# RWKV attention with a top-1 expert router: the order of rows and maskings in the attention's steps, and the attention's end written out step by step

## The chip, the core and the metric

The kernel runs on one core of a Trainium2 chip. The metric is the time of one execution on the device in microseconds. Before the change it is 439.42 us, the median of three runs (438.77 to 440.31). The profile is of one further execution, whose span is 438.4 us.

A core has five engines that work side by side, each with its own instruction queue, kept in order: TensorE (PE; the loads of its weights are shown apart as PEld), VectorE (DVE), ScalarE (ACT), GpSimd (POOL) and SyncE (SP), which starts transfers. Results of TensorE land in PSUM; everything else lives in SBUF. An engine that waits holds up all that stands behind it in its queue, so the order in which a program lists its operations is part of its speed.

## What is computed

Inputs are r, k, v of shape (4, 8, 768, 48) (batch, heads, sequence, head size), a decay w and a bonus u per head and channel. The attention is a recurrence over the sequence; its rows, 3072 of 384, then go through a router that sends each to one of eight experts.

```python
for t in range(S):
    kt, vt, rt = k[:, :, t], v[:, :, t], r[:, :, t]
    cur = einsum('bhd,bhe->bhde', u[None] * kt, vt)
    y[:, :, t] = einsum('bhd,bhde->bhe', rt, state + cur)
    state = w[None, :, :, None] * state + einsum('bhd,bhe->bhde', kt, vt)
x = y.transpose(0, 2, 1, 3).reshape(B * S, H * D)          # (3072, 384)

xn, en = x / (norm(x) + 1e-6), expert_emb / (norm(expert_emb) + 1e-6)
logits = xn @ en.T / tau
expert_idx = argmax(logits); gate_w = softmax(logits)[expert_idx]
for e in range(E):                                          # E = 8, F = 1024
    mask = expert_idx == e
    out[mask] = gate_w[mask, None] * (relu(x[mask] @ w1[e]) @ w2[e])
```

## The kernel before

The sequence is cut into six chunks of 128 positions; a unit is one chunk of one batch, 24 units in all. The loop below runs over the units; each pass works on several of them at different stages. Inside a unit the attention is matrix work: scores (`at`) of all pairs of positions, masked to the earlier ones (`AT`); sums (`y`) of the values weighted by the masked scores and, from the second chunk on, of the state that is carried from chunk to chunk (`st`, `state`); the term of the bonus u, which is a row scaling of v (`diag`, `xd`). `rows` turns the sums back (`yrows`) and adds `xd` to them: that is `X`, the rows that the router and the experts take. Heads go in pairs of 64 rows, of which 48 are used; the 16 rows between are the gaps that the diff speaks of.

```python
B, H, S, D = 4, 8, 768, 48
C, NCH, DP, NP, PP = 128, 6, 64, 4, 112        # PP = DP + D
...

def own_rows(k, i, half):
    if half == 0:
        k.xd[i] = k.work.tile([128, H, D], F32, name="xd", tag="xd")
    diag, V = k.diag[i], k.loaded[i][2]
    for h in range(half * H // 2, (half + 1) * H // 2):
        k.nc.scalar.mul(k.xd[i][:, h, :], V[:, h, :], diag[:, h : h + 1])

def turn_k(k, i):
    nc = k.nc
    Kw = k.Kpad[i % len(k.Kpad)]
    kt = k.ps.tile([128, NP, C], F32, name="kt", tag="tp")
    for p in range(NP):
        nc.tensor.transpose(kt[:, p, :], pair(Kw, p), k.ident)
    k.KT[i] = k.work.tile([128, NP, C], F32, name="KT", tag="KT")
    nc.scalar.copy(k.KT[i], kt)

def scores(k, i):
    nc = k.nc
    RT, KT = k.RT[i], k.KT.pop(i)
    at = [k.ps.tile([128, NP, C], F32, name="at", tag="at") for _ in range(2)]
    for p in range(NP):
        for s in range(2):
            rows = slice(s * DP, s * DP + D)
            nc.tensor.matmul(at[s][:, p, :], KT[rows, p, :], RT[rows, p, :], start=True, stop=True)
    k.AT[i] = []
    for s in range(2):
        a = k.work.tile([128, NP, C], F32, name=f"AT{s}", tag=f"AT{s}")
        nc.vector.tensor_mul(a, at[s], k.umask[:, None, :].to_broadcast([128, NP, C]))
        k.AT[i].append(a)

...

def sums(k, i):
    nc = k.nc
    mm = nc.tensor.matmul
    c, b = divmod(i, B)
    V, RT, AT, T = k.loaded[i][2], k.RT.pop(i), k.AT.pop(i), k.state[b]
    y = [k.ps.tile([128, NP // 2, C], F32, name="y", tag="y") for _ in range(2)]
    for q in range(NP // 2):
        for u in range(2) if c > 0 else ():
            for s in range(2):
                mm(
                    y[s][u * DP : (u + 1) * DP, q, :], T[s * DP : s * DP + D, 2 * q + u, :],
                    RT[s * DP : s * DP + D, 2 * q + u, :], start=(q == 0), stop=False, skip_group_check=True,
                )
    for s in range(2):
        for q in range(NP // 2):
            for u in range(2):
                p = 2 * q + u
                mm(
                    y[s][u * DP : u * DP + D, q, :], V[:, 2 * p + s, :], AT[s][:, p, :],
                    start=(c == 0 and q == 0), stop=True, skip_group_check=True,
                )
        yT = k.yT[i % len(k.yT)]
        if c > 0:
            nc.scalar.copy(yT[0:PP, s], y[s][0:PP])
        else:
            for u in range(2):
                heads = slice(u * DP, u * DP + D)
                nc.scalar.copy(yT[heads, s], y[s][heads])
    if b == 0:
        k.groups[c] = group(k, c)

def rows(k, i):
    nc = k.nc
    c, b = divmod(i, B)
    yT = k.yT[i % len(k.yT)]
    y = k.ps.tile([128, 2, NP // 2, 2 * DP], F32, name="yrows", tag="tp")
    for s in range(2):
        for q in range(NP // 2):
            nc.tensor.transpose(y[:, s, q, 0:PP], yT[0:PP, s, q, :], k.ident[0:PP, 0:PP])
    def by_bank(t):
        return t.rearrange("t (g s) d -> t s g d", s=2)
    X = k.groups[c].X[:, b, :].rearrange("t (h d) -> t h d", d=D)
    nc.vector.tensor_add(
        by_bank(X), y.rearrange("t s q (u d) -> t s (q u) d", d=DP)[:, :, :, 0:D], by_bank(k.xd.pop(i))
    )
```

PSUM tiles come from pools with few buffers: two each for the tags `tp`, `at` and `y`, one for every other tag.

After each chunk its 512 rows are routed: logits, the choice of an expert, the place of each row in its expert's list (`ranks`, `places`), the list entries (`gates`, `listed`, `taken`, `summed`). After the fourth chunk the two experts with the most rows are settled, their weights loaded and the first 128 rows of each gathered, so that these two tiles (`Early`) can be computed while the last two chunks are routed. The loop runs seven passes past the last unit, in which the stages of the last chunks drain and the early tiles are worked off in halves:

```python
def attention(k):
    units = B * NCH
    def on(f, i, *more):
        if 0 <= i < units:
            f(k, i, *more)
    ...                                        # of_group, whole: the same by units and by chunks of a group
    for i in range(-1, units + 7):
        j = i - SETTLED * B                    # SETTLED is 3
        ...
        on(turn_r, i + 1)
        on(own_rows, i, 0)
        on(turn_k, i + 1)
        whole(turn_logits, i - 3)
        on(scaled, i + 2)
        for n in (0, 1) if i < 0 else (i + 2,):
            on(own, n)
        on(states, i)
        of_group(squares, i - 1)
        on(own_rows, i, 1)
        whole(norms, i - 2)
        whole(choose, i - 3)
        whole(before, i - 3)
        whole(exps, i - 4)
        whole(located, i - 4)
        whole(gates, i - 5)
        whole(listed, i - 5)
        on(own_sum, i + 1)
        if j == 10:
            k.lists = turned_lists(k, perm, "st")
            lists = taken_by_rank(k, k.lists)
            first = [Early(k, r, *lists, w) for r, w in zip(LAST, k.weights)]
        on(sums, i)
        on(carry, i)
        on(scores, i + 1)
        on(rows, i)
        of_group(put, i)
        of_group(turn_rows, i - 1)
        whole(logits, i - 2)
        whole(ranks, i - 3)
        if i == units:
            first[0].hidden(0)
        whole(taken, i - 5)
        ...
        if j == 7:
            load_, count = loads(k, "st")
        if j == 8:
            settle(k, load_, count)
            for w, r in zip(k.weights, LAST):
                load_weights(k, expert_number(k, r), w)
        if j == 9:
            perm = turner(k, k.by)
        if j == 10:
            to = outs(k, lists[0], E * TM)
        ...         # passes past the last unit, and what follows: see the diff

class Early:        # its rows are gathered when it is made
    ...
    def turn(self):
        k, nc = self.k, self.k.nc
        ps = k.ps.tile([128, NK, 128], F32, name="early_x", tag="tp")
        for m in range(NK):
            nc.tensor.transpose(ps[:, m, :], self.G[:, m * 128 : (m + 1) * 128], k.ident)
        self.xT = k.work.tile([128, NK, 128], F32, name="earlyx", tag="KU")
        nc.vector.tensor_copy(self.xT, ps)
    ...             # hidden, rows, out: see the lines taken away in the diff
```

When all lists are known (`lists`, `taken_by_rank`), the rest of each expert's rows is gathered and the experts run one after the other (`experts`, not changed).

## Time and profile before

| what | value |
|---|---|
| time, median of three | 439.42 us |
| span of the profile | 438.4 us |
| TensorE busy | 404.5 us, 92% |
| first scores start | 15.27 us |
| scores of the last unit start | 147.41 us |
| first transpose of the experts' rows (L1055) | 188.81 us |
| last gathers of early rows land, early_x starts | 155.09 and 156.51 us |

The page gives the busy time of each engine, the span in 40 slices, the transfers and the chain that ended last. In its forty slices, with the engines' busy share in tenths, three regimes can be told apart: the attention up to slice 14 (each slice is 11 us), the end of the attention with the early tiles up to slice 17, and the experts:

```profile
PE   8889999999998877998999999999999999999960
...
ACT  2477776666677610133323323143233233232110
POOL 6875677676755210440032140222221231300200
PEclk9999999999999969999999999999999999999995
```

A busy TensorE isn't a TensorE at its peak, and a wait that is listed for an engine is put down to whichever releaser came last by the profile; where the engine named had long been done, it was another one. In a timeline, "xN" at the end of a line merges N instructions, and the bracket says how long the engine idled before it and what ended the idling.

### The profile page before, as it was taken

The numbers are of one execution on the slowest core, as the hardware profiler recorded it, in microseconds if no ns is written. First come the engines' busy times: TensorE is split into PE (matmuls) and PEld (weight loads), VectorE is DVE, ScalarE is ACT, GpSimd is POOL, SyncE is SP. The second block draws the span as 40 slices with busy tenths as digits, with TensorE's granted clock in tenths as the row PEclk, the third lists the DMA queues.
The fourth block names the chain that finished last, engine by engine and source line by source line (L and its number), as shares of the span: only waits on it lengthen the run. The fifth ranks groups of instructions, "written<-read, shape, count | busy, mean of one in ns | idle before, by whom it ended". The sixth has DMA issues, their size and how long they took to land.

```text
span 438.4 us, 9319 instructions
## 1 busy us (share of the span) xinstructions
PE 404.5 (92%) x3556; PEld 357.2 (81%) x3556; DVE 251.0 (57%) x610; ACT 176.6 (40%) x531; POOL 161.4 (37%) x218
## 2 busy tenths in 40 slices
PE   8889999999998877998999999999999999999960
PEld 3667778787887764878999999999999999899660
DVE  4566776767678723255776776355556566566210
ACT  2477776666677610133323323143233233232110
POOL 6875677676755210440032140222221231300200
PEclk9999999999999969999999999999999999999995
DMA  8966656666641980234452643155155151230110
GB/s 165 180 145 145 141 122 139 130 129 145 144 93 42 365 299 1 67 94 146 146 175 65 234 138 144 37 167 175 59 167 196 37 165 52 63 135 2 52 41 21
DMA packets 93801, 54.40 MB, mean 124 GB/s; under 512 B 76937, under 2 KB 88380, under 8 KB 93746
## 3 DMA queue, kind: packets, MB, share of 16 engines
q1 hardware_dynamic: 89024, 43.85, 37.5%
q0 software_dynamic: 3296, 9.44, 6.7%
q8 instruction: 30, 0.49, 0.4%
q10 hardware_dynamic: 1426, 0.41, 0.4%
q14 instruction: 25, 0.20, 0.2%
HBM read 44.45 MB, written 9.63 MB: 123 GB/s over the span
## 4 chain that ended last, share of the span: by engine, by line
PE 77%; DVE 7%; POOL 4%; ACT 4%; issue 3%; DMA 2%; POOLq 0%; DVEq 0%; ACTq 0%
PE ps L1107 22%; PE ps L1171 16%; PE ps L1211 5%; PE at L344 4%; PE ps L1224 4%; PE y L400 3%; PE early_h L920 3%; PE wake L67 3%; DVE AT L348 2%; PE ps L1085 2%; PE ps L1055 2%; PE kt L332 2%; PE early_y L931 2%; PE y L392 2%; PE st L363 2%
## 5 line engine op out<-in xcount | busy, mean ns | idle before, releaser
L1231 POOL DMA_INDIRECT out_dram<-y,to x25 | 30.0, 1200 | 179.5 <-issue 93.1
L1107 PE MATMUL ps<-xTe,w 128*128 128x192 f32 (+3 forms) x336 | 62.9, 327 | 0.0
L1107 PEld LDWEIGHTS ps<-xTe,w 128*128 128x128 f32 x336 | 55.9, 190 | 0.4
L312 ACT ACTIVATE xd<-V,diag 128x48 f32<-128x48 f32 x192 | 48.3, 325 | 0.2 <-DVE diag L303 0.2
L348 DVE TENSOR_TENSOR AT<-at,umask 128x512 f32<-128x512 f32 x48 | 30.9, 686 | 29.4 <-PE at L344 29.4
L1114 ACT ACTIVATE hT<-hT 128x384 f32<-128x384 f32 (+3 forms) x42 | 22.0, 523 | 33.8 <-DVE hT L1137 21.1
L1171 PE MATMUL ps<-Tw,Sh 128*128 128x192 f32 x192 | 32.5, 326 | 0.0
L1171 PEld LDWEIGHTS ps<-Tw,Sh 128*128 128x128 f32 x192 | 31.4, 190 | 0.0
L973 POOL DMA_INDIRECT G<-xs,take x25 | 27.1, 1083 | 8.8 <-issue 3.4
L344 PE MATMUL at<-RT,KT 48*128 48x128 f32 x384 | 27.9, 284 | 2.0 <-DVE RT L323 0.9
L1107 PE MATMUL ps<-Tx,Sw 128*128 128x192 f32 (+3 forms) x168 | 29.6, 326 | 0.0
L344 PEld LDWEIGHTS at<-RT,KT 48*128 48x128 f32 x384 | 23.3, 187 | 6.6 <-ACT xd L312 2.8
L1107 PEld LDWEIGHTS ps<-Tx,Sw 128*128 128x128 f32 x168 | 27.6, 190 | 0.1
L400 PE MATMUL y<-AT,V 128*48 128x128 f32 x384 | 25.8, 277 | 0.0
L1124 DVE TENSOR_TENSOR u<-ps,p 128x384 f32<-128x384 f32 (+3 forms) x14 | 7.8, 556 | 31.4 <-PE ps L1107 30.6
L511 ACT COPY xT<-xp 128x384 f32<-128x384 f32 x24 | 11.5, 479 | 35.2 <-PE xp L509 35.2
L297 POOL TENSOR_TENSOR KU<-KU,Rpad 128x384 f32<-128x384 f32 x24 | 24.1, 1003 | 1.9
L296 POOL TENSOR_TENSOR KU<-K,u_bc 128x384 f32<-128x384 f32 x24 | 24.1, 1002 | 0.0
L288 POOL TENSOR_TENSOR Kpad<-K,kpow 128x384 f32<-128x384 f32 x23 | 23.0, 999 | 2.8 <-DVE kpow L101 2.8
L1171 PE MATMUL ps<-w,hT 128*128 128x192 f32 x128 | 23.4, 326 | 0.0
L400 PEld LDWEIGHTS y<-AT,V 128*48 128x48 f32 x384 | 19.8, 123 | 3.4 <-issue 3.4
L1171 PEld LDWEIGHTS ps<-w,hT 128*128 128x128 f32 x128 | 21.3, 190 | 0.3
(240 smaller groups left out, 816.6 us busy)
## 6 DMA issues: line engine op xcount, KB each, us to landing
w<-in_moe_w_dram SPq DMA_DIRECT2D x16, 1536.0 KB, 6.8
K<-in_k_dram SPq DMA_DIRECT2D x24, 192.0 KB, 4.1
V<-in_v_dram SPq DMA_DIRECT2D x24, 192.0 KB, 4.3
xs<-X SPq DMA_DIRECT2D x24, 192.0 KB, 2.0
Rpad<-in_r_dram SPq DMA_DIRECT2D x23, 192.0 KB, 4.2
G<-xs,take POOLq DMA_INDIRECT x27
out_dram<-y,to POOLq DMA_INDIRECT x25
Rpad<-in_r_dram ACTq DMA_DIRECT2D x1, 192.0 KB, 4.2
```

Of the source, the lines that this page charges most:

```text
L288: k.nc.gpsimd.tensor_mul(k.Kpad[i % len(k.Kpad)][:, :, 0:D], k.loaded[i][0], k.kpow)
L296: nc.gpsimd.tensor_mul(KU, K, k.u_bc)
L297: nc.gpsimd.tensor_mul(KU, KU, R[:, :, 0:D])
L312: k.nc.scalar.mul(k.xd[i][:, h, :], V[:, h, :], diag[:, h : h + 1])
L344: nc.tensor.matmul(at[s][:, p, :], KT[rows, p, :], RT[rows, p, :], start=True, stop=True)
L348: nc.vector.tensor_mul(a, at[s], k.umask[:, None, :].to_broadcast([128, NP, C]))
L400: mm(y[s][u * DP : u * DP + D, q, :], V[:, 2 * p + s, :], AT[s][:, p, :], start=(c == 0 and q == 0), stop=True, skip_group_check=True,)
L973: nc.gpsimd.indirect_dma_start(out=G[0:n, :], out_offset=None, in_=k.xs[:, :], in_offset=IndirectOffsetOnAxis(ap=take[0:n], axis=0), bound ...
L1107: nc.tensor.matmul(ps[:, j, :], weights[:, (f + j) * 128 : (f + j + 1) * 128], moving, start=(first and j == 0), stop=True, skip_group_che ...
L1114: nc.scalar.activation(h, h, ACT.Relu)
L1171: nc.tensor.matmul(ps, a[:, f, :], b[:, f, :], start=(first and f == 0), stop=(f == NF // 2 - 1), skip_group_check=True)
L1231: k.nc.gpsimd.indirect_dma_start(out=k.out[:, :], out_offset=IndirectOffsetOnAxis(ap=k.to[0:here, j : j + 1], axis=0), in_=y[0:here, :], i ...
```

## The change

It has five parts.

1. The masking of the scores, one vector operation per set of heads, leaves `scores` and becomes `masked`. The pass now lists: scores of the next unit, its first masking, the rows of this unit (`rows`, with the addition that makes X), the second masking. The addition stood behind both maskings before; the purpose is to read the transposed rows out of PSUM earlier.
2. The gaps between heads: the state tiles shrink from 64 to 48 columns per pair, and products that write 48 of 64 rows now take 64 columns of the operand (the next head's first columns) where the gap would otherwise stay unwritten. So in the first chunk, too, one copy per bank reads all 112 rows, where there were two per bank.
3. The last unit's scaling `xd` is one product on GpSimd, made a pass earlier, instead of eight on ScalarE.
4. The loop ends with the last unit. What followed in seven further passes is written out in the order wanted.
5. The early tiles become a generator of single steps (three products into one slice of `hT`, or one product of the output rows); `fill(n)` puts n of them between two stages of routing. ScalarE scales the early rows, not VectorE.

```diff
--- before.py
+++ after.py
...
@@ -312,6 +312,11 @@
         k.nc.scalar.mul(k.xd[i][:, h, :], V[:, h, :], diag[:, h : h + 1])
+def own_rows_once(k, i):
+    k.xd[i] = k.work.tile([128, H, D], F32, name="xd", tag="xd")
+    k.nc.gpsimd.tensor_mul(k.xd[i], k.loaded[i][2], k.diag[i][:, :, None].to_broadcast([128, H, D]))
@@ -342,11 +347,13 @@
...
-    k.AT[i] = []
-    for s in range(2):
-        a = k.work.tile([128, NP, C], F32, name=f"AT{s}", tag=f"AT{s}")
-        nc.vector.tensor_mul(a, at[s], k.umask[:, None, :].to_broadcast([128, NP, C]))
-        k.AT[i].append(a)
+    k.at[i] = at
+def masked(k, i, s):
+    a = k.work.tile([128, NP, C], F32, name=f"AT{s}", tag=f"AT{s}")
+    k.nc.vector.tensor_mul(a, k.at[i][s], k.umask[:, None, :].to_broadcast([128, NP, C]))
+    k.AT.setdefault(i, []).append(a)
@@ -359,9 +366,9 @@
     st = k.ps.tile([128, NP, D], F32, name="st", tag="st")
     for p in range(NP):
         for s in range(2):
-            h = 2 * p + s
+            h, n = 2 * p + s, (DP, D)[s]
             nc.tensor.matmul(
-                st[s * DP : (s + 1) * DP, p, :], Kw[:, h, :], V[:, h, :], start=True, stop=True, skip_group_check=True
+                st[s * DP : s * DP + n, p, :], Kw[:, h, 0:n], V[:, h, :], start=True, stop=True, skip_group_check=True
             )
     k.st[i] = st
...
@@ -385,29 +392,27 @@
     mm = nc.tensor.matmul
     c, b = divmod(i, B)
     V, RT, AT, T = k.loaded[i][2], k.RT.pop(i), k.AT.pop(i), k.state[b]
+    V, T = (a.rearrange("q h d -> q (h d)") for a in (V, T))
     y = [k.ps.tile([128, NP // 2, C], F32, name="y", tag="y") for _ in range(2)]
     for q in range(NP // 2):
         for u in range(2) if c > 0 else ():
             for s in range(2):
+                p, n = 2 * q + u, (DP, D)[u]
                 mm(
-                    y[s][u * DP : (u + 1) * DP, q, :], T[s * DP : s * DP + D, 2 * q + u, :],
-                    RT[s * DP : s * DP + D, 2 * q + u, :], start=(q == 0), stop=False, skip_group_check=True,
+                    y[s][u * DP : u * DP + n, q, :], T[s * DP : s * DP + D, p * D : p * D + n],
+                    RT[s * DP : s * DP + D, p, :], start=(q == 0), stop=False, skip_group_check=True,
                 )
     for s in range(2):
         for q in range(NP // 2):
             for u in range(2):
-                p = 2 * q + u
+                p, n = 2 * q + u, DP if c == 0 and u == 0 else D
+                h = 2 * p + s
                 mm(
-                    y[s][u * DP : u * DP + D, q, :], V[:, 2 * p + s, :], AT[s][:, p, :],
+                    y[s][u * DP : u * DP + n, q, :], V[:, h * D : h * D + n], AT[s][:, p, :],
                     start=(c == 0 and q == 0), stop=True, skip_group_check=True,
                 )
         yT = k.yT[i % len(k.yT)]
-        if c > 0:
-            nc.scalar.copy(yT[0:PP, s], y[s][0:PP])
-        else:
-            for u in range(2):
-                heads = slice(u * DP, u * DP + D)
-                nc.scalar.copy(yT[heads, s], y[s][heads])
+        nc.scalar.copy(yT[0:PP, s], y[s][0:PP])
...
@@ -805,7 +810,7 @@
             f(k, k.groups[i // B])
     emb = build_experts(k)
-    for i in range(-1, units + 7):
+    for i in range(-1, units):
         j = i - SETTLED * B
@@ -815,7 +820,8 @@
         on(turn_r, i + 1)
-        on(own_rows, i, 0)
+        if i < units - 1:
+            on(own_rows, i, 0)
         on(turn_k, i + 1)
         whole(turn_logits, i - 3)
         on(scaled, i + 2)
@@ -823,7 +829,8 @@
         on(states, i)
         of_group(squares, i - 1)
-        on(own_rows, i, 1)
+        if i < units - 1:
+            on(own_rows, i, 1)
@@ -832,6 +839,8 @@
         whole(gates, i - 5)
         whole(listed, i - 5)
         on(own_sum, i + 1)
+        if i == units - 2:
+            own_rows_once(k, i + 1)
         if j == 10:
             k.lists = turned_lists(k, perm, "st")
@@ -839,13 +848,13 @@
         on(sums, i)
         on(carry, i)
         on(scores, i + 1)
+        on(masked, i + 1, 0)
         on(rows, i)
+        on(masked, i + 1, 1)
         of_group(put, i)
         of_group(turn_rows, i - 1)
         whole(logits, i - 2)
-        if i == units:
-            first[0].hidden(0)
         whole(taken, i - 5)
@@ -863,28 +872,51 @@
             perm = turner(k, k.by)
         if j == 10:
             to = outs(k, lists[0], E * TM)
-        if i == units - 1:
-            for f in first:
-                f.turn()
-        if i == units + 1:
-            first[0].hidden(1)
-        if i == units + 2:
-            first[0].rows(0)
-        if i == units + 4:
-            first[0].rows(1)
-            load_, _ = loads(k, "xp")
-            first[0].out(to)
-            first[1].hidden(0)
+    g, h = k.groups[NCH - 2], k.groups[NCH - 1]
+    early = itertools.chain(*(f.steps(to) for f in first))
+    def fill(count):
+        for _ in range(count):
+            next(early, None)
+    gates(k, g)
+    first[0].turn()
+    turn_rows(k, h, B - 1)
+    listed(k, g)
+    squares(k, h, B - 1)
+    norms(k, h)
+    logits(k, h)
+    first[1].turn()
+    logits_out(k, h)
+    fill(1)
+    turn_logits(k, h)
+    choose(k, h)
+    before(k, h)
+    taken(k, g, "tp")
+    fill(2)
+    ranks(k, h)
+    load_, _ = loads(k, "xp")
+    places(k, h)
+    exps(k, h)
+    located(k, h)
+    summed(k, g)
     by = order(k, load_, k.settled)
-    lists = turned_lists(k, turner(k, by), "xp")
-    first[1].hidden(1)
+    perm = turner(k, by)
+    gates(k, h)
+    listed(k, h)
+    fill(4)
+    taken(k, h, "tp")
+    summed(k, h)
+    fill(1)
+    lists = turned_lists(k, perm, "xp")
     k.take, k.gates = taken_by_rank(k, lists)
     k.rows_of = {r: gathers(k, r) for r in LAST}
     k.to = outs(k, k.take, E * TM)
-    first[1].rows(0)
-    first[1].rows(1)
-    first[1].out(to)
     caps_passed(k, load_, by)
+    for _ in early:
+        pass
 class Early:
@@ -911,35 +943,31 @@
         self.xT = k.work.tile([128, NK, 128], F32, name="earlyx", tag="KU")
         nc.vector.tensor_copy(self.xT, ps)
-    def hidden(self, half):
-        k, nc = self.k, self.k.nc
-        ps = k.ps.tile([128, NF // 2, 128], F32, name="early_h", tag="at")
-        fs = slice(half * NF // 2, (half + 1) * NF // 2)
-        for j, f in enumerate(range(fs.start, fs.stop)):
+    def steps(self, to):
+        k, nc, half = self.k, self.k.nc, NF // 2
+        for f in range(NF):
+            if f % half == 0:
+                ps = k.ps.tile([128, half, 128], F32, name="early_h", tag="at")
             for m in range(NK):
                 nc.tensor.matmul(
-                    ps[:, j, :], self.weights[0][:, m, f * 128 : (f + 1) * 128], self.xT[:, m, :],
+                    ps[:, f % half, :], self.weights[0][:, m, f * 128 : (f + 1) * 128], self.xT[:, m, :],
                     start=(m == 0), stop=(m == NK - 1),
                 )
-        nc.scalar.activation(self.hT[:, fs, :], ps, ACT.Relu)
-
-    def rows(self, half):
-        k = self.k
-        if half == 0:
-            self.ps = k.ps.tile([128, DM], F32, name="early_y", tag="y")
-        for f in range(half * NF // 2, (half + 1) * NF // 2):
-            k.nc.tensor.matmul(
-                self.ps, self.hT[:, f, :], self.weights[1][:, f, :], start=(f == 0), stop=(f == NF - 1)
-            )
-
-    def out(self, to):
-        k, nc, ps = self.k, self.k.nc, self.ps
-        y = k.work.tile([128, DM], F32, name="earlyy", tag="xd")
-        nc.vector.tensor_scalar_mul(y, ps, self.gate)
-        nc.gpsimd.indirect_dma_start(
-            out=k.out[:, :], out_offset=IndirectOffsetOnAxis(ap=to[:, self.col], axis=0), in_=y[:, :], in_offset=None,
-            bounds_check=N - 1, oob_is_err=False,
-        )
+            if f % half == half - 1:
+                nc.scalar.activation(self.hT[:, f - half + 1 : f + 1, :], ps, ACT.Relu)
+            yield
+        ps = k.ps.tile([128, DM], F32, name="early_y", tag="y")
+        for f in range(NF):
+            nc.tensor.matmul(ps, self.hT[:, f, :], self.weights[1][:, f, :], start=(f == 0), stop=(f == NF - 1))
+            if f == NF - 1:
+                y = k.work.tile([128, DM], F32, name="earlyy", tag="xd")
+                nc.scalar.mul(y, ps, self.gate)
+                nc.gpsimd.indirect_dma_start(
+                    out=k.out[:, :], out_offset=IndirectOffsetOnAxis(ap=to[:, self.col], axis=0), in_=y[:, :],
+                    in_offset=None, bounds_check=N - 1, oob_is_err=False,
+                )
+            yield
...
```

More of the change, by code (lines that the diff above doesn't have):

```diff
@@ L138, in build_consts @@
     for b in range(B):
-        t = k.aconst.tile([128, NP, DP], F32, name=f"state{b}")
+        t = k.aconst.tile([128, NP, D], F32, name=f"state{b}")
         nc.gpsimd.memset(t, 0.0)
@@ L374, in carry @@
         return
-    part = T[:, :, 0:D]
-    nc.vector.tensor_add(part, part, st)
-    nc.gpsimd.tensor_mul(part, part, k.wC)
+    nc.vector.tensor_add(T[0:PP], T[0:PP], st[0:PP])
+    nc.gpsimd.tensor_mul(T[0:PP], T[0:PP], k.wC[0:PP])
 def sums(k, i):
@@ L652, in listed, with taken @@
     g.lane, g.what = slices(k, g.c, k.slots.rearrange("p e t -> p (e t)"), *g.spots)
-def taken(k, g):
-    g.take = k.ps.tile([2 * QS, 128], F32, name="take", tag="st")
+def taken(k, g, tag="st"):
+    g.take = k.ps.tile([2 * QS, 128], F32, name="take", tag=tag)
     for b in range(B):
@@ L1443 @@
     n.Rpad, n.Kpad, n.state = [], [], []
-    for name in ("loaded", "KU", "diag", "xd", "RT", "KT", "AT", "st", "y", "groups"):
+    for name in ("loaded", "KU", "diag", "xd", "RT", "KT", "at", "AT", "st", "y", "groups"):
         setattr(n, name, {})
```

## The prediction

> **What bounds the kernel now.** I read the page first, then the waits of TensorE from 38 to 189 us, then the timeline of single steps, and last the tail with its clock. The page's first part says that TensorE is the engine to watch:
>
> ```profile
> PE 404.5 (92%) x3556; PEld 357.2 (81%) x3556; DVE 251.0 (57%) x610; ACT 176.6 (40%) x531; POOL 161.4 (37%) x218
> ```
>
> From 189 us on nothing in the experts is edited, so the 249.6 us from there to the end (438.4 - 188.8) move as one block. All is decided before. There PE idles little; the waits, whose columns are total us, times and longest, are:
>
> ```profile
> PE early_x L910 <- DMA G<-xs,take: 1.9, 2, 1.4
> PE kt L332 <- DVE X L429: 1.9, 3, 0.6
> PE rank L578 <- DVE seq L556: 1.3, 1, 1.3
> PE yrows L423 <- ACT yT L406: 1.3, 1, 1.3
> PE kt L332 <- POOL KU L297: 1.1, 2, 0.6
> PE take L658 <- POOL what L643: 1.0, 1, 1.0
> PE kt L332 <- DVE at L585: 0.9, 4, 0.2
> ```
>
> The three rows of kt sum to 3.9 us over nine steps, and are one wait. The timeline of a plain step (start, duration, engine) shows it:
>
> ```profile
> 60.60 0.60 PE L423 MATMUL yrows<-ident,yT 112*128 112x112 f32 x4
> 60.70 1.29 DVE L348 TENSOR_TENSOR AT<-at,umask 128x512 f32<-128x512 f32 x2 [1.35 <-PE at L344]
> ...
> 61.37 0.60 PE L321 MATMUL rt<-ident,Rpad 128*128 128x128 f32 x4
> ...
> 61.90 0.55 DVE L429 TENSOR_TENSOR X<-yrows,xd 128x384 f32<-128x384 f32 x1
> ...
> 62.59 0.63 PE L332 MATMUL kt<-ident,Kpad 128*128 128x128 f32 x4 [0.63 <-DVE X L429]
> ```
>
> The tag tp has two PSUM buffers and three users per step (rt, kt, yrows), so kt takes the buffer of the yrows before it and needs X to have read that. X stands behind both maskings AT; it ends at 62.45 and kt starts 0.14 us later. At 109.81 the view names POOL's KU, but X ended at 109.66 there: the same wait. Where logits or lists lie between (lgT 0.8 us, take 0.6 us), PE arrives later and waits for nothing.
>
> In the first chunk another wait rules: four copies of yT instead of two.
>
> ```profile
> 30.59 1.53 ACT L410 COPY yT<-y 48x256 f32<-48x256 f32 x4
> ...
> 32.17 0.41 PE L423 MATMUL yrows<-ident,yT 112*128 112x112 f32 x2 [0.37 <-ACT yT L410]
> ```
>
> The tail's clock (columns: stretch, length, busy us of PE, PEld, DVE, ACT, POOL, granted clock, DMA share, GB/s):
>
> ```profile
> 152.00:154.00 2.00, 1.01 (x7) 0.71 (x7) 0.52 (x1) 1.17 (x6) 0.00 (x0) 1.00 1.02 404
> 154.00:156.00 2.00, 0.90 (x3) 0.50 (x3) 0.03 (x1) 0.73 (x3) 0.00 (x0) 0.52 1.03 396
> 156.00:158.00 2.00, 1.49 (x7) 1.52 (x8) 1.14 (x3) 0.00 (x0) 0.00 (x0) 0.50 1.03 373
> 158.00:160.00 2.00, 2.00 (x12) 2.00 (x11) 1.19 (x5) 0.48 (x1) 0.65 (x2) 0.50 1.07 372
> 160.00:162.00 2.00, 2.00 (x15) 1.94 (x14) 0.00 (x0) 0.00 (x0) 1.10 (x2) 0.77 0.97 345
> ```
>
> PE pauses for the gathered early rows, comes back at half speed, and needs until about 161. DMA is full with the experts' weights there.
>
> **What the skill says.** "TensorE: Matmul & The Clock Gate", section "What's actually happening": the clock is halved after an idle window of some 3.4 us and needs about as long a busy one to come back. The trace agrees: 0.52 and 0.50 after the pause, full again from 162. Its "Part 4: PE-mode transpose" adds that transposes don't count as busy in the same way, and all of PE's work from 151.4 to 157.6 is transposes. "GPSIMD Engine Reference", "1. Specifications": no PSUM access, and SBUF interfaces shared with VectorE. The product moved to POOL has both inputs in SBUF, so it can go there; the same form takes 1.00 us (L296). "Perfetto Trace Analysis", "Optimization Strategy": a bubble that repeats can mean too few buffers for the next tile. The tp bubble is this; the change releases the buffer earlier instead of adding one.
>
> **The change part by part.**
>
> *X between the maskings.* AT takes 0.69 us alone and the next vector op starts about 0.55 us after it, so in the step above X can start when yrows is there, at 61.30, instead of 61.90, and ends at 61.85; kt starts at 61.99. By PE's own pace (0.49 us after rt's start, as at 121.12 and 121.61) it could at 61.86: 0.13 us stays. So the four plain steps (three of 0.63, and 109.81) gain 0.50 each, the four with rank (0.23 each) all of it, as PE comes later there, and that at 133.41 0.45: 2.0 + 0.9 + 0.45 = 3.4 us. The second masking ends where X ended; it is wanted 2.4 us later. PE is then the bound: work between score starts is 5.86 - 0.63 = 5.23 us. ACT has a loop beside it: xT, four xd, KT, squares, four xd, two yT, then PE's yrows and xp. By the starts of consecutive ops that is about 5.0 us. It fits, barely. POOL has 3.5 us per step plus at most 1.2, DVE under 5.
>
> *First chunk.* Two copies of 112 rows take 0.62 to 0.74 us, four of 48 took 1.52. A copy of 48 rows costs what one of 112 does (0.367 against 0.362 us), so this halves. Tracking the step starts: kt at 22.44 moves to 21.83 by X; yrows of the next unit, whose second half ended at 27.05, ends at 25.7 (gain 1.35); those after are set by ACT's loop of 5.0 us where they took 5.5: ends at 30.6 (was 32.58) and 35.5 (was 38.11). kt at 38.93 then starts at 36.2: gain 2.7 us. The weights of 64 instead of 48 columns for half of these sums are loaded under other matmuls.
>
> *Narrow states.* Half of the 16 weight loads of st have 48 columns for 64. 20 steps, estimated at 0 to 0.05 us each: 0.4 us. Additions and products keep their 192 columns: nothing.
>
> *Rows of the last unit on POOL.* Eight scalings (0.32 us each) leave ACT; before, PE waited 1.28 us for yT behind four of them. Yet the next PE work is early_x, which waits for the gather. POOL's product needs diag (ends at 148.0) and stands ahead of the gathers: the first is issued at about 149.07 instead of 148.62. So 1 us is won ahead of a wait, and the wait ends 0.45 us later.
>
> *The tail.* Its work is the same: 32 early steps of 0.69 us (3 matmul sums of 0.23, or one of 0.69), 22 us, plus the routing. From the gather's landing (155.1) to the first expert transpose (188.8) PE idled 0.5 + 0.4 + 0.8 + 1.3 + 1.0 + 0.7 = 4.7 us. In the new order I count: 0.45 for the copy xT ahead of lgT, no wait for lg, seq or the fourth chunk's list, 2.4 ahead of the last take, 0.6 at the end. The 2.4 comes from DVE: rank is read at 164.2, then 0.3 + 0.45 + 0.6 + 0.25 + 0.3 + 0.65 + 0.5 + 0.55 + 0.95 us of loads, places, exps, spots, summed, order, perm, gates and slices, and 0.95 on POOL, gives 169.5, while four filled steps last until 167.0. So 3.5 us idle for 4.7, minus the gather's 0.45, and real matmuls now come between transposes while the clock is low, perhaps 0.6 more at half speed. Tail: 0.1 us gained.
>
> **Sum.** 2.7 + 3.4 + 0.4 + 0.1 = 6.6 us; 439.4 - 6.6 = 432.8 us, 1.5% less.
>
> **Rivals.** (1) ACT becomes the bound of the steps. Its loop of 5.0 us against 5.23 leaves 0.2; if starts slip, yrows waits and a third of the 3.4 goes: 434. For it: ACT already stands with no pause from squares to yT. Against: it waits 0.3 us for kt in each step, which shrinks. (2) The tail gives more: if PE, without the gap at 151.4 to 152.7, keeps its clock, some 3 us of half speed vanish and the time is 429.5. Against: the pause itself moves from 1.4 to 2.7 us at one place. (3) The tail gives it back: a low clock for one window longer (1.7 us), or the later gathers under 400 GB/s of weights landing late: 435. (4) DVE's settling at 138 to 141, which kept the scores at 141.75 waiting 0.91 us for RT, could grow if it starved take or lists; I see the same amount of DVE work there, so nothing.
>
> **Range and chances.** Of the 6.6 us, 6.1 rest on waits read off directly, with about 1 us of doubt each for chunk 0 and the steps; the tail has about 2. Together some 2.7 us: 432.8, 429.2 to 436.4. Faster by 2% means under 430.6, which needs the tail to give over 2 us: 0.22. Slower by 2% would need a new serial wait: 0.03.
>
> **What would show it.** kt's wait for X at or under 0.15 us per step; score starts 5.2 to 5.3 us apart in plain steps; ACT's yT twice 0.36 us from the first unit, and kt of the fifth step near 36.2; the scores of the last unit near 141.0 instead of 147.4; early_x first at 149.2 or so, about 8.1 us after them (7.7 before); the last take waiting some 2 us for what; the first expert transpose near 182.2. I am wrong if yrows waits for yT in every step, if the clock in the tail is not low or low for longer, or if PE waits for the rows of the last unit from POOL.

## The result, and the profile after

The changed kernel takes 428.86 us in the median of four runs (428.64 to 430.65), the kernel before 439.87 in the runs beside it. The ratio is 0.976, with a 95% interval of 0.972 to 0.980. The prediction was 432.8 us with a range of 429.2 to 436.4: the median lies 0.3 us below the range's lower end, and 11.0 us were gained where 6.6 were expected.

The first line of the page (busy time, share and instructions of each engine) shows that TensorE has as many instructions as before and that its pauses are fewer: 27 us of the span are not busy, where it was 34:

```profile
PE 399.8 (94%) x3556; PEld 355.6 (83%) x3556; DVE 251.1 (59%) x608; ACT 171.5 (40%) x517; POOL 161.8 (38%) x219
```

The waits of TensorE between 38 and 180 us (total, times, longest) have no row of kt left. In the tail the waits for seq (1.3 us) and for lgT (0.8 us) are gone too, and the wait of take for what has grown from 1.0 to 2.0 us:

```profile
PE early_x L942 <- DMA G<-xs,take: 2.2, 1, 2.2
PE take L663 <- POOL what L648: 2.0, 1, 2.0
PE at L349 <- ACT yT L415: 1.0, 1, 1.0
PE yrows L428 <- ACT yT L415: 1.0, 1, 1.0
PE ps L1083 <- ACT earlyy L965: 0.7, 1, 0.7
```

The timeline of a plain step shows X between the maskings, and kt 0.65 us after the start of rt, where it was 1.22:

```profile
55.62 0.69 DVE L355 TENSOR_TENSOR AT<-at,umask 128x512 f32<-128x512 f32 x1 [0.88 <-PE at L349]
...
56.22 0.56 DVE L434 TENSOR_TENSOR X<-yrows,xd 128x384 f32<-128x384 f32 x1
56.28 0.60 PE L326 MATMUL rt<-ident,Rpad 128*128 128x128 f32 x4
...
56.70 0.68 DVE L355 TENSOR_TENSOR AT<-at,umask 128x512 f32<-128x512 f32 x1
...
56.93 0.63 PE L337 MATMUL kt<-ident,Kpad 128*128 128x128 f32 x4
```

In the first chunk two copies of 112 rows stand where four of 48 stood, and one group of transposes follows them:

```profile
27.83 0.63 ACT L415 COPY yT<-y 112x256 f32<-112x256 f32 x2
...
28.24 0.68 PE L428 MATMUL yrows<-ident,yT 112*128 112x112 f32 x4
```

The clock of the tail (stretch, length, busy us of PE, PEld, DVE, ACT, POOL, granted clock, DMA share, GB/s) is low for half as long as before:

```profile
146.00:148.00 2.00, 1.22 (x12) 0.79 (x12) 0.71 (x2) 0.39 (x2) 0.00 (x0) 1.00 1.02 383
148.00:150.00 2.00, 1.85 (x20) 1.37 (x21) 0.65 (x2) 0.87 (x4) 1.27 (x3) 0.50 1.06 371
150.00:152.00 2.00, 2.00 (x16) 1.83 (x16) 0.75 (x2) 0.00 (x0) 0.48 (x1) 0.64 1.07 374
152.00:154.00 2.00, 2.00 (x24) 1.83 (x18) 1.36 (x8) 0.00 (x0) 0.00 (x0) 1.00 0.58 212
```

Starts in the timelines give the stages, in us:

| stage | before | after | difference |
|---|---|---|---|
| start to the first scores | 15.27 | 13.95 | -1.32 |
| to the scores of unit 5 (chunk 0) | 26.43 | 23.73 | -2.70 |
| to the scores of unit 23 (steps) | 105.71 | 100.79 | -4.92 |
| to early_x | 7.69 | 8.23 | +0.54 |
| to the first expert transpose | 33.71 | 30.72 | -2.99 |
| to the end (experts) | 249.59 | 249.38 | -0.21 |
| span | 438.4 | 426.8 | -11.6 |

The start of early_x is that of its first transposes, at 155.10 us before; those of the second early tile start at 156.51 there. The first row is not the change's. TensorE's warm-up products, whose number is not edited, load weights in 0.34 us at first and in 0.19 later; the last slow load starts at 6.91 us in the profile before and at 4.35 in the one after. Over the fourteen profiles of this study the first scores start between 13.93 and 15.52 us, in the main later where the slow loads end later. So 11.6 us is a lucky pair, and the medians' 11.0 is the better figure.

### The profile page after: what moved, and what is told of

Its sections match the earlier page's. It is cut to its first block, busy times and chain, and to the rows that moved or that the text cites. A ratio compares the mean times of both kernels' runs of the same rounds, so it can differ in the third digit from the quotient of the medians.

```text
span 426.8 us, 9300 instructions
## 1 busy us (share of the span) xinstructions
PE 399.8 (94%) x3556; PEld 355.6 (83%) x3556; DVE 251.1 (59%) x608; ACT 171.5 (40%) x517; POOL 161.8 (38%) x219
## 5 line engine op out<-in xcount | busy, mean ns | idle before, releaser
L312 ACT ACTIVATE xd<-V,diag 128x48 f32<-128x48 f32 x184 | 46.3, 326 | 0.4 <-DVE diag L303 0.4
L355 DVE TENSOR_TENSOR AT<-at,umask 128x512 f32<-128x512 f32 x48 | 32.9, 686 | 23.1 <-PE at L349 23.1
L410 PE MATMUL y<-AT,V 128*48 128x128 f32 (+1 forms) x384 | 26.2, 277 | 0.0
L410 PEld LDWEIGHTS y<-AT,V 128*48 128x48 f32 (+1 forms) x384 | 20.2, 124 | 3.4 <-issue 3.4
```

What stands on the lines that cost most here:

```text
L355: k.nc.vector.tensor_mul(a, k.at[i][s], k.umask[:, None, :].to_broadcast([128, NP, C]))
L410: mm(y[s][u * DP : u * DP + n, q, :], V[:, h * D : h * D + n], AT[s][:, p, :], start=(c == 0 and q == 0), stop=True, skip_group_check=True,)
```

## The experiments

Each ratio is against the kernel before in runs on the same chip, with its 95% interval. Stages are of one profile each, and repeat to 0.1 us where the clock is steady.

**The three parts alone.** The first kernel has only the order of X and the maskings:

```diff
         on(scores, i + 1)        # without the maskings
+        on(masked, i + 1, 0)
         on(rows, i)
+        on(masked, i + 1, 1)
```

> Edit: in the kernel before, only X is put between the two maskings. Theory (the start-to-start loss): the wait of kt cost more than the idle time that the view lists, because TensorE's results end some 0.17 us after its next work could have started; measured start to start, rt to kt took 1.22 us in a plain step and 0.87 in one with ranks, and 0.65 and 0.47 after. So scores of unit 5 to scores of unit 23 (105.7 us before) should take about 101.2, that is 4.5 us less, and the time should fall by 4.5 to 5.5 us with the 0.6 won in the first chunk. Rival (the listed idle time, as in the prediction): 3.4 us less in that stretch. The end, from the last scores to the first expert transpose, stays at 41.4 us but for the clock's luck.

Ratio 0.990 (0.987 to 0.992), median 435.3 us. The steps take 101.13 us, 4.58 less than before: the start-to-start count, and not the 3.4 of the listed idle. The sum of rt's start to kt's start over the nineteen steps falls from 14.53 to 10.07 us, that is by 4.46. The waits of this kernel show what is left; the rows of kt are gone, and those of the tail are as before except that take doesn't wait:

```profile
PE early_x L914 <- DMA G<-xs,take: 1.9, 2, 1.5
PE rank L580 <- DVE seq L558: 1.3, 1, 1.3
PE yrows L425 <- ACT yT L408: 1.3, 1, 1.3
PE at L344 <- ACT yT L408: 1.0, 1, 1.0
PE lg L542 <- ACT lgT L536: 0.8, 1, 0.8
```

The second has only the written gaps and the narrow states:

```diff
-        if c > 0:
-            nc.scalar.copy(yT[0:PP, s], y[s][0:PP])
-        else:
-            for u in range(2): ...
+        nc.scalar.copy(yT[0:PP, s], y[s][0:PP])
```

> Edit: in the kernel before, only the gaps between heads are written and the states are narrowed. Theory: the first chunk's four copies become two, and its steps become about 0.5 to 0.7 us shorter each; first scores to scores of unit 5 falls from 26.4 us by about 2.2. Narrower weight loads give 0.03 us per later step, 0.5 us in all (after took 1.15 from kt to the state sums where before took 1.17). Time: 2.5 us less. Rival: half of the gain in the first chunk comes from X's place, so gaps alone give only 1.3 us there.

Ratio 0.998 (0.997 to 0.999), median 439.17 us. Chunk 0 takes 25.30 us, 1.13 less: the rival. The later steps take 105.37, 0.34 less, so the narrow loads are worth what was estimated. The two stages make 1.47 us, of which the ratio shows only 0.7; where the rest went isn't shown. Why chunk 0 gives so little alone is in its waits between 15 and 40 us. No yrows waits for the copies of yT any more, and kt waits for X, which stands behind both maskings:

```profile
PE kt L332 <- DVE X L427: 1.2, 2, 0.6
PE kt L332 <- DVE cum L195: 0.6, 1, 0.6
PE kt L332 <- DVE ent L231: 0.5, 1, 0.5
```

In the kernel with the maskings alone it is the other way about; yrows waits for the four copies there, and 0.56 us are won in chunk 0:

```profile
PE yrows L425 <- ACT yT L412: 1.5, 5, 0.4
```

Together the two win 2.70 us there, and 1.0 of that exists only when both are done.

The third has the end written out, the early tiles in steps and the last unit's rows on GpSimd, with the order of the maskings and the gaps as before:

> Edit: in the kernel before, only the last unit's rows on GpSimd and the written-out end with the early tiles in steps. Last scores to first expert transpose took 41.4 us before and 38.95 after. Theory (clock): the order alone gives little, 0 to 0.5 us, and what was gained is the shorter stretch at half clock (about 4 us instead of 7), which depends on the phase of the clock's window and need not repeat: this stretch takes 39 to 41.5 us here, and the granted clock tells which. Rival (order): the new order itself gives the 2.4 us, and the stretch is 38.9 us whatever the clock does.

Ratio 0.995 (0.993 to 0.996), over nineteen runs, median 437.3 us: 2.4 us. The end takes 38.96 us, 2.44 less. Both theories had a share: the clock was low for 3.4 us here and 6.8 before, and from early_x on TensorE is idle for 2.98 us instead of 4.71. The table further down tells how much is whose.

**The last take.** `fill(7)` stands where `fill(4)` did:

> Edit: in the changed kernel, seven early steps instead of four stand ahead of the last take, and so three fewer in the rest. Theory: TensorE's wait of 2.0 us for the list entries there is filled with work that is needed anyway; 1.9 us less than the changed kernel, about 427.0. Rival: the lists, and so the gathers of the first expert's rows, come no earlier, and they or the last early product set the end anyway: same time as the changed kernel.

Ratio 0.974 (0.971 to 0.977), median 428.57 us, which can't be told from the changed kernel's. In its profile the wait is gone:

```profile
PE early_x L942 <- DMA G<-xs,take: 2.1, 1, 2.1
...
PE yrows L428 <- ACT yT L415: 1.0, 1, 1.0
PE ps L1083 <- ACT earlyy L965: 0.7, 1, 0.7
```

and early_x to the first expert transpose takes 29.83 us, 0.89 less than in the changed kernel, although the clock was low twice as long (6.8 us against 3.4). TensorE's idle time in this stretch fell from 2.98 to 0.79 us and its busy time rose from 27.74 to 29.05. So the wait was on the path, and the clock took part of its worth back.

**Is it the clock?** Products that nobody reads are put where TensorE waits, two ahead of the last unit's rows and three or five ahead of the early tiles' transposes:

```diff
+def held(k, count):
+    ps = k.ps.tile([128, NP * C], F32, name="hold", tag="at")
+    for _ in range(count):
+        k.nc.tensor.matmul(ps, k.ones, k.rpow.rearrange("q p c -> q (p c)"), start=True, stop=True)
```

> Edit: the kernel before, with five products of 128x128 by 128x512 added whose result nobody reads, two ahead of the last unit's rows and three ahead of the early tiles' transposes, 2.2 us of work where TensorE waited 1.3 and 1.4 us. They keep it busy, so that the clock should not drop. Theory (clock): in the kernel before, two windows of 3.41 us at half clock cost up to 3 us; here the stretch from the last scores to the first expert transpose falls from 41.4 to about 38.5, and the granted clock stays at 1.00 from 150 to 162. Rival (order alone): the low clock lies beside waits and costs nothing, and the stretch stays at 41 or grows by what the added products delay.

Ratio 0.998 (0.996 to 1.000), median 439.09 us. The products took 0.86 us each, twice what I had counted, and early_x starts 9.05 us after the last scores (7.69 without them). From there to the first expert transpose it takes 31.34 us, 2.37 less: 1.5 of that are waits which the later start of early_x took away, and 0.9 is busy time of TensorE. The clock did stay at 1.00 from 144 to 168, and then fell for one window behind the wait for seq:

```profile
166.00:168.00 2.00, 0.45 (x3) 0.29 (x3) 1.21 (x8) 0.20 (x2) 0.00 (x0) 1.00 0.00 0
168.00:170.00 2.00, 2.00 (x6) 1.41 (x7) 1.33 (x9) 0.13 (x1) 0.00 (x0) 0.53 0.00 0
170.00:172.00 2.00, 2.00 (x5) 1.14 (x4) 1.32 (x5) 0.10 (x1) 0.34 (x1) 0.62 0.00 0
```

The same in the changed kernel:

> Edit: the changed kernel, with seven such products that nobody reads, two ahead of the last unit's rows (wait of 1.0 us) and five ahead of the first early transposes (wait of 2.2 us). Theory (clock): the one window at half clock goes, and the stretch from the last scores to the first expert transpose falls from 38.95 to about 37.5; against the kernel before with the same hold (38.5 expected) that leaves 1.0 us for the new order at equal clock. Rival (order): the difference at equal clock is the whole 2.4 us.

Ratio 0.982 (0.978 to 0.985), median 431.6 us: slower, as early_x starts at 10.74 instead of 8.23. Behind that the clock is at 1.00 throughout, and the rest takes 29.15 us instead of 30.72. One window is thus worth 1.6 us, and not because the later start took waits away: the idle time of TensorE is the same, and all of the difference is in its busy time. From early_x to the first expert transpose, in us:

| kernel | length | TensorE busy | idle | clock low (from the last scores on) |
|---|---|---|---|---|
| before | 33.71 | 29.00 | 4.71 | 6.8 |
| the new end alone | 30.80 | 27.82 | 2.98 | 3.4 |
| changed | 30.72 | 27.74 | 2.98 | 3.4 |
| changed, seven products | 29.15 | 26.17 | 2.98 | none |
| changed, `fill(7)` | 29.83 | 29.05 | 0.79 | 6.8 |

So of the 2.99 us between the profiles before and after, 1.73 are fewer waits and 1.26 are the clock. The kernel before with products still had a window in its stretch, so times of the two orders at full clock can't be set side by side.

A smaller hold, one product at each place:

> Edit: the changed kernel, with two products that nobody reads (0.86 us each, 0.43 us per half as the view counts them), one ahead of the last unit's rows and one ahead of the first early transposes; nothing else is moved. The larger hold of seven products delayed early_x by 2.5 us and hid what the clock was worth. Theory (clock): early_x starts 8.2 us after the last scores as in the changed kernel, and from there to the first expert transpose it takes 29.2 us instead of 30.7, at a granted clock of 1.00; 37.4 us from the last scores (38.95 in the changed kernel), and the time over several runs falls to about 427.3. Rival: two products are too few in this order, the clock drops once, and the stretch stays at 38.9.

Ratio 0.977 (0.975 to 0.980), median 429.76 us: no gain, and the stretch is 39.14 us. That is the rival's result, but not for its reason. The clock did not fall behind the first wait, but behind the wait of 2.0 us for the last take, which the hold does not fill:

```profile
156.00:158.00 2.00, 0.75 (x7) 0.56 (x6) 1.67 (x9) 0.00 (x0) 0.05 (x1) 1.00 0.00 0
158.00:160.00 2.00, 1.23 (x13) 1.05 (x14) 0.29 (x1) 0.00 (x0) 0.72 (x2) 1.00 0.00 0
160.00:162.00 2.00, 2.00 (x8) 1.39 (x7) 1.25 (x9) 0.60 (x1) 0.65 (x1) 0.55 0.00 0
```

The tail has two waits behind which the clock can fall, and this hold fills one. The second wait does not always bring a fall: it is 2.02 us long in the kernel with seven products too, and there the clock stayed at 1.00. The last section shows what decides.

**The last unit's rows and the gathers.** In one kernel GpSimd's product follows the two gathers; in another it is undone, and ScalarE makes the rows again in eight scalings:

```diff
-        if i == units - 2:
-            own_rows_once(k, i + 1)
         if j == 10:
             ...
             first = [Early(k, r, *lists, w) for r, w in zip(LAST, k.weights)]
+        if i == units - 2:               # left out in the kernel with ScalarE's rows
+            own_rows_once(k, i + 1)
```

> Edit: the changed kernel, with GpSimd's product for the last unit's rows behind the two gathers of the early rows instead of ahead of them. Theory (as predicted: the product delays the gather by 0.45 us): the gathers start 0.7 us after the last scores instead of 1.75, early_x starts 7.3 to 7.6 us after them instead of 8.2, and the time falls by 0.6 to 0.9 us; X of the last unit comes no later, as its product ends 4.6 us after the last scores. Rival: the gathers land when the 400 GB/s of weights let them, so early_x starts no sooner and nothing changes.

> Edit: the changed kernel with the last unit's rows made by eight scalings on ScalarE again, that is, without its third part. Theory: the 1 us that the product wins lies ahead of the wait for the gathered rows, so the third part gains nothing and costs 0.5 to 0.8 us of the gather's start; this kernel is as fast or 0.6 us faster than the changed one. Rival: the last unit's rows are on the path, and this kernel is about 1 us slower.

Ratios 0.979 (0.976 to 0.982) and 0.979 (0.975 to 0.983), medians 430.4 and 430.9 us. In both early_x starts 7.7 us after the last scores: the 0.5 us is real. But neither is faster. Both profiles have two low windows, one behind each wait, and the stretch from early_x takes 31.5 and 32.1 us. Their medians are 1.5 and 2.0 us above the changed kernel's, which the intervals don't separate. On time alone the third part is thus neither shown to help nor to cost; what it costs the gather is shown. With the gathers first there was a surprise besides. A small VectorE operation takes 1.44 us there, and ends when GpSimd's product ends. It takes 0.26 in the changed kernel, and 0.19 in the kernel with ScalarE's rows, where it starts equally long (0.48 us) after the second gather but no product follows:

```profile
142.14 1.44 DVE L992 SCALAR_TENSOR_TENSOR to<-batch,to 128x32 int32<-128x32 int32 x1
142.67 0.85 POOL L317 TENSOR_TENSOR xd<-V,diag 128x384 f32<-128x384 f32 x1
143.50 0.18 DVE L590 TENSOR_TENSOR at<-rank,seq 128x32 f32<-128x32 f32 x1
...
144.47 0.23 ACT L604 ACTIVATE l<-l 128x32 f32<-128x32 f32 x1 [2.58 <-DVE l L603]
144.60 0.63 ACT L415 COPY yT<-y 112x256 f32<-112x256 f32 x2
```

The exponential waits for VectorE's chain, and yT, whose sums were ready at 142.8, stands behind it. So the next kernel moves the exponential:

```diff
-        whole(exps, i - 4)
+        if i < units - 1:
+            whole(exps, i - 4)
 ...
+    exps(k, g)
     gates(k, g)
     first[0].turn()
```

> Edit: the changed kernel with the two gathers of early rows ahead of GpSimd's product for the last unit's rows, and with the exponential of the fifth chunk's logits moved behind the last unit's rows. Why: with the gathers first, early_x did start 0.5 us sooner after the last scores (7.71 against 8.23), but a small VectorE operation of 0.19 us took 1.44, until GpSimd's product ended, and ScalarE's exponential and then yT waited for it in order. Theory (order on ScalarE and VectorE): with the exponential out of the way, yrows starts 4.2 to 5.2 us after the last scores instead of 6.2, X is there before the gathered rows, and early_x to the first expert transpose takes 30.0 to 30.8 us with one low window of the clock, so the stretch is 37.7 to 38.5 us (changed kernel 38.95). Rival: the gathers' landing leaves early_x at 7.7, and what follows waits for the second gather or the list entries, so the stretch stays at 38.9 or above.

Ratio 0.978 (0.976 to 0.979), median 430.24 us. yrows starts 4.61 us after the last scores instead of 6.18, so the order on ScalarE was the cause. It brings nothing here: TensorE waits 2.1 us for the gathered rows all the same, and the clock was low for 6.8 us. The stretch is 39.47 us, the rival's result, by another way than it said.

**Together.** The late exponential, the gathers first and seven filled steps:

> Edit: as the kernel with the late exponential, and seven early steps instead of four ahead of the last take. Theory: both add up; the wait of 2.0 us for the list entries is filled (1.0 to 1.9 us) and the early rows come 0.5 us sooner; 426.5 to 427.5 us, under the changed kernel's 428.9. Rival: the clock's low windows make up for it, and no more than 0.5 us is left.

Ratio 0.973 (0.971 to 0.975), median 428.47 us over six runs from 425.5 to 430.0: the rival. The profile has 6.8 us of low clock:

```profile
146.00:148.00 2.00, 0.46 (x2) 0.46 (x3) 0.74 (x5) 0.23 (x1) 0.00 (x0) 0.78 1.03 393
148.00:150.00 2.00, 2.00 (x20) 1.21 (x22) 1.36 (x3) 0.88 (x3) 0.08 (x1) 0.50 1.04 380
150.00:152.00 2.00, 2.00 (x23) 1.53 (x16) 0.00 (x0) 0.38 (x3) 1.68 (x3) 0.50 1.07 374
152.00:154.00 2.00, 2.00 (x13) 1.67 (x14) 0.99 (x4) 0.00 (x0) 0.00 (x0) 0.51 1.06 381
```

And with one product at each of the two places of the hold:

> Edit: as the combined kernel, with two products of 128x128 by 128x512 (0.86 us each, as measured in the kernels with the hold) whose result nobody reads, one ahead of the last unit's rows and one ahead of the first early transposes. Theory: they fit into the waits there and keep TensorE busy enough for the clock to stay at 1.00, which is worth 1.2 to 1.6 us per low window: 425 to 426 us. Rival: two are too few, the clock drops all the same, and the time is that of the combined kernel.

Ratio 0.970 (0.968 to 0.972), median 426.38 us. The same stretch:

```profile
146.00:148.00 2.00, 0.93 (x6) 0.43 (x5) 0.96 (x6) 0.39 (x2) 0.00 (x0) 1.00 1.03 396
148.00:150.00 2.00, 1.78 (x31) 1.15 (x29) 1.36 (x3) 1.09 (x4) 0.40 (x2) 1.00 1.02 373
150.00:152.00 2.00, 2.00 (x21) 1.66 (x20) 1.30 (x5) 0.16 (x1) 1.35 (x2) 1.00 1.08 376
152.00:154.00 2.00, 2.00 (x21) 2.00 (x20) 0.96 (x8) 0.00 (x0) 0.00 (x0) 1.00 1.06 381
```

From the last scores to the first expert transpose it takes 34.93 us (7.69 to early_x and 27.24 from it), 2.73 less than without the hold and 4.02 less than in the changed kernel. These two idle products are the whole edit, and the gain is in the clock: from early_x on TensorE is busy for 26.22 us instead of 29.08 and idle for 1.02 instead of 0.80. Single runs say the same by their mean granted clock. Five of the six without the hold had 0.979 or 0.980 and took 427.8 to 430.0 us, and one had 0.986 and took 425.5; five of the six with it had 0.985 to 0.987 and took 425.4 to 426.5, and one had 0.983 and took 428.7. The median is 2.1 us under the combined kernel's, 2.5 under the changed one's and 13.4 under that of the kernel before beside it; the intervals of the ratios overlap a little with the first and just touch the second.

## Why the prediction was right, and where it was off

The direction and the causes of the first three terms held, and the sum fell short by 4.4 us in the medians: 1.2 us of it in the steps, and 2.3 us in the tail, where a term had the wrong sign.

*First chunk.* Predicted 2.7, measured 2.70. kt of the fifth step, expected near 36.2, starts at 34.94, which is 36.26 with the later start of before. The working moved X first and yT after it; that 1.0 us of the gain needs both, it did not say, and the single parts show it.

*X between the maskings.* Mechanism right, size off: 3.4 predicted, 4.58 measured alone. The step that failed is the one that took the wait from the list, "three of 0.63 [...], the four with rank (0.23 each) all of it". The listed idle begins where the last result of rt ends, 0.60 us after rt's start in the plain step, but TensorE's own pace from rt to kt is 0.49, so kt could have started 0.1 to 0.2 us before that. Start to start, rt to kt took 1.22 in a plain step and takes 0.65, so 0.57 was won and not 0.50 (the prediction's own times, 62.59 and 61.99, give 0.60; it took the 0.13 us that count from TensorE's own pace off the listed 0.63); in a step with ranks it took 0.87 and takes 0.47, so 0.40 and not 0.23; the step at 133.41 took 1.09 and takes 0.50. Four, four and one of them: 2.3 + 1.6 + 0.6 = 4.5. The 0.13 us expected to stay is 0.16. Score starts in plain steps lie 5.25 us apart; 5.2 to 5.3 was said.

*Narrow states.* 0.4 predicted, 0.34 measured.

*ACT as the bound* (the first rival) did not come: no wait for yT remains in the ordinary steps, only 1.0 us at the scores behind the settling, where 0.91 was lost before. The name of the releaser there is ScalarE's, but RT is finished at 132.68 and the scores start at 132.83: the old wait for RT, the fourth rival, unchanged in kind.

*Rows of the last unit.* "1 us is won ahead of a wait, and the wait ends 0.45 us later": early_x starts 0.54 us later, and sooner again when the gathers go first.

*The tail.* The term that was furthest off: 0.1 predicted, 2.45 measured in the pair of profiles and 2.4 over nineteen runs of the tail alone. The waits after early_x were counted as 3.5 us for 4.7; the list has 0.22 + 2.02 + 0.73, that is 3.0. The failed step is "perhaps 0.6 more at half speed". The profile of before had two low windows and the changed one's had one, and TensorE's busy time for the same products fell from 29.00 to 27.74 us: 1.3 won where 0.6 was to be lost. Of 2.45 us, then: 1.7 from fewer waits, 0.5 lost at the gather, and 1.3 from the clock. The second rival was thus half true, though its reason was not: it is not that the first pause got shorter. Nineteen runs make a lasting gain of 2.4 us for the new end as a whole; how often each order meets one window or two is not settled. The eleven of them with a mean clock of 0.984 to 0.986 took 437.0 us in the mean, the seven at 0.981 or 0.982 took 438.2, and one at 0.977 took 439.7. But the fifteen runs of the kernel before at 0.982 to 0.984 took 439.8, and the twenty-three at 0.977 to 0.980 took 440.1, so there the higher clock went with 0.2 us alone. That mean also counts the low clock after TensorE's last work, so it can't be turned into a number of windows, and the clock's share of the 2.4 us is measured in the pair of profiles alone. A time under 430.6 us had a chance of 0.22 and "needs the tail to give over 2 us", which it did, beside 1.2 us more from the steps.

*Sum.* Of the 11.0 us, the terms on record were 2.7, 3.4, 0.4 and 0.1; measured 2.7, 4.6, 0.3 and 2.4, sum 10.0. By the ratios of the runs, the three parts alone gave 4.5, 0.7 and 2.4, and 1.0 needs two of them: 8.6 us, where the ratio's interval allows 9.0 to 12.2 for the whole. The last 1 to 2 us are thus not assigned to a part; the start, which varied by 1.6 us between the profiles, can hold some of them.

## What to carry to other kernels

Size a repeated TensorE wait by the distance between starts, with and without it, and not by the idle time that a view lists; here the list was 3.9 us and the loss 4.5. When two waits stand one behind the other in the same step, curing one shows the other, so try the cures together before judging either. Where TensorE has pauses of about 2 us between stages, look at the granted clock behind each of them. Fill all of them, with wanted work first and with idle products where none is at hand: here filling the second alone left 6.8 us of low clock behind the first, and shortening the first alone left 3.4 us behind the second. Compare such kernels over several runs, since the same pause cost 1.6 us in some profiles and nothing in others.

## What the runs showed of the hardware

The low clock comes in pieces. In every profile with a fall in the tail, the stretches of 2 us add up to 3.4 us of half clock or to two times that: before 0.48/0.5 x 2 + 2 + 2 + 0.23/0.5 x 2 = 6.8 us, after 2 + 0.36/0.5 x 2 = 3.4. The Trainium skill, "TensorE: Matmul & The Clock Gate", section "What's actually happening", states a free-running window of 3413 ns; the runs agree. In each profile all low stretches, that after TensorE's last product included, start on one grid of 3.413 us (in the profile after at 148.01 and 417.67 us, 79 intervals apart). One piece costs 1.6 us in this dense work (29.15 against 30.72 us), two cost 2.7 (34.93 against 37.66), and in the profile the two hold products, 1.7 us of TensorE's time in waits, were enough to prevent two pieces.

The grid also shows when the clock falls. The fourteen profiles have fifteen falls before TensorE's last product, each at the end of a grid interval in which TensorE was idle for 1.67 to 2.40 us in all; after an interval with 1.48 us or less it did not fall. The wait of 2.02 us for the last take lies in one interval in three profiles (with the gathers first from 156.23 to 158.25 us, interval 155.51 to 158.93), and the clock fell at the end of it each time. In the four others that have this wait a boundary of the grid divides it (with seven products 159.12 to 161.15, boundary at 160.10), and the clock did not fall. Idle time is not the whole measure, though: in the interval that holds the last product of all, 1.88 to 1.99 us of it brought no fall in four profiles. The prediction took from the same section that an idle window of some 3.4 us halves the clock, and said that the trace agrees; but the interval ahead of its fall at 154.09 held 1.67 us of idle time in two pauses, and the measurement decides. All this is read off these profiles, and no run was made to test it.

A VectorE operation of some 0.2 us can be held until a GpSimd product beside it ends: it took 1.43 or 1.44 us, ending within 0.1 us of the product's end, in all four kernels in which the product follows the gathers. "GPSIMD Engine Reference", section "1. Specifications", says that the two share their SBUF interfaces and that VectorE operations of some kinds contend with GpSimd, among them those with two SBUF inputs, as this one has; the size of the wait is from these runs.
